# A Fourier-mixing and squared-ReLU kernel: a load issued later, a small tile in another PSUM pool, and six more pair steps without their third matmul pass

## Chip, cores and metric

The kernel runs on one core of a Trainium2 chip. The metric is the device time of one execution in microseconds; the time given for a kernel is the median of its runs. The engines are TensorE (PE, with its weight loads PEld), VectorE (DVE), ScalarE (ACT), GpSimd (POOL) and SyncE (SP). The last two only issue DMAs here, apart from some small set-up work and a few tiny copies on POOL. ScalarE also issues a few DMAs. "The queue" of an engine is its list of instructions, which it works off in order.

## What is computed

```python
# x: (8, 3008, 256), w_in: (256, 2048), w_out: (2048, 256), all float32
X = np.fft.fft(x, axis=1)
X = np.fft.fft(X, axis=2)
y = X.real.astype(np.float32).reshape(8 * 3008, 256)
h = np.maximum(y @ w_in, 0.0)
out = h * h @ w_out
```

## The kernel before

**The mathematics.** The transform along the 256 model dimensions is folded into `w_in` once, at the start: `gh[:, 0]` holds the cosine part, `gh[:, 1]` the sine part and `gh[:, 2]` is −2 times `gh[:, 1]`, one of its 128 rows (model dimension 0) being left at zero. The transform along the sequence is made with cosine and sine tables on TensorE, after "folds" on VectorE have used its symmetries. Its results are `zc` and `zs`. Rows k and S − k of the result share these: one is p + q, the other p − q, where p = `gh[:, 0]` · `zc` and q = `gh[:, 1]` · `zs`. So only half of the rows, 12,040 columns, are carried, and each column gives two rows of the output.

**Windows.** The columns are cut into 25 windows, numbered 0 to 24, in the order of the outer loop (L680). Window 0 has 240 columns, windows 2 and 3 have 376, window 5 has 448, the last has 360, all others 512. The fifth window is number 4.

**Pair steps.** A window has 8 steps, one for each pair of 128-wide chunks of the 2048 hidden features. A plain step does this: `pq` (L726) makes p + q in PSUM (L730, L731: four matmuls); `square` (L738) takes ReLU on ScalarE (L740) into a buffer `h1`, of which there are three, and squares it on VectorE (L745), or on ScalarE (L743) where the step is in `by_act`; `turn` (L733) adds −2q to the same PSUM tile (L736: two matmuls, the "third pass"); a second `square` handles the mirrored rows. So a plain step has six matmuls of 512 columns.

**Halved steps.** A step in the set `two` has no third pass. `half_q` (L751) makes q alone (L755: two matmuls), and ScalarE copies −2q to `sn` (L758). `half_p` (L760) adds p (L764: two matmuls), ScalarE copies p + q to `hd` (L767), and VectorE does the rest: a correction row times a weight (L769, twice), two additions (L770, L771), the ReLU (L773) and the square (L774) over both halves. The correction row `eb` is row 0 of `zs`, which `row_spread` (L574) sends to DRAM from ScalarE's queue (L579) and brings back to all 128 partitions from SP's queue (L581). It is issued in the last step of the window before, behind the stores that SP already has. There are two `sn` buffers, and two `hd` buffers for each of two names.

**The plan.** `plan(w)` (L666) gives the halved steps and the `by_act` steps of a window. `PLAN[4]` halves steps 1, 2, 4, 5 and gives ScalarE the first square of 0, 3, 6. `PLAN[3]` halves 1, 3, 5 and gives ScalarE 2, 4, 6. `PLAN[0]` does neither; windows 0, 1, 2 and 4 have it.

**What else runs in a step.** Between its parts each step calls `others` (L776), which runs three sorts of work.

- The second matmul `ffn2_steps` (L602) of the window before: 16 groups of 8 matmuls of 256 columns (L618), two groups a step in a full window. They read the tile `h2` that the squares wrote. Their PSUM tile `po` is in the pool `ps_o` (two banks); ScalarE copies it out (L633), and SP stores it (L598).
- The products `z_steps` (L460) for the next window: matmuls into `pz` in the pool `ps_z` (two banks), copies on ScalarE (L485, L489), and a last `scalar_tensor_tensor` on VectorE (L496), which finishes `zc` or `zs` and frees the bank.
- The folds of the batches to come. For the batch in place i, `d_even` and `n_cos` run in the window in `first_at`, steps 0 and 2 (L713). `d_odd`, `n_sin`, `odds`, `even`, `back` and `nyq` run in the next window, the one in `fold_at` (L702), and the four `late` jobs in the one in `late_at` (L710), at steps 3 to 6.

| windows | first part of a fold | second part | late part | plan before |
|---|---|---|---|---|
| 9, 12, 15, 18 | yes | | yes | 3 |
| 5, 8, 10, 13, 16, 19 | | yes | | 3 |
| 6, 21 | | | yes | 4 |
| 7 | yes | | | 4 |
| 3, 11, 14, 17, 20, 22, 23, 24 | | | | 4 |
| 4 | yes | | of the batch in place 1 | 0 |

**DMAs of a fold.** `load_x` (L118) brings a batch, 3 MB, into the one tile `xo` with one to two direct DMAs and two or three gathers, all from POOL's queue. For the last two places, some of them wait for another's landing (L143, L149). In the kernel before, `d_odd` calls it for the next batch as soon as it has read the tile (L356), in step 0 of the window in `fold_at`. In the same window `even` writes `scr` to DRAM at step 5 (L383), and `back` reads it back into `rb` at step 6 (L391, L393), in the same queue of POOL, behind the load. `nyq` (L372) runs after step 7: two tiny matmuls into `py`, a tile of the pool `ps_o`, and a copy by VectorE (L377).

**Pairs.** A window that has 512 columns after one of fewer than 384 treats its steps two by two (`ng` = 2, L790). Windows 1 and 4 are such.

Of the kernel before, what the change touches and what calls it, by code (L numbers as in the profile page):

```python
# [8 lines left out]
F32 = mybir.dt.float32  # L9
F16 = mybir.dt.float16  # L10
# [5 lines left out]
P = 128  # L16
# [12 lines left out]
def kernel(  # L29
# [15 lines left out]
    B, S, D = x.shape  # L45
# [9 lines left out]
    WN = 512  # L55
# [4 lines left out]
    PLAN = {4: ((1, 2, 4, 5), (0, 3, 6)), 3: ((1, 3, 5), (2, 4, 6)), 2: ((1, 4), (0, 3, 6)), 0: ((), ())}  # L60
# [42 lines left out]
    tmp = ctx.enter_context(tc.tile_pool(name="tmp", bufs=2))  # L103
# [9 lines left out]
    ps_o = ctx.enter_context(tc.tile_pool(name="ps_o", bufs=2, space=bass.MemoryType.PSUM))  # L113
# [52 lines left out]
    xs = {0: load_x(0)}  # L166
# [117 lines left out]
    at = const.tile([P, 2, P + 1], F32, name="at")  # L284
# [51 lines left out]
    def fold_steps(i):  # L336
# [16 lines left out]

        def d_odd():
            nc.vector.tensor_tensor(fof[:, :, 1:129], lo, hi, op=ALU.subtract)
            if i + 1 < B:  # L356
                xs[i + 1] = load_x(i + 1)

        def n_cos():
# [11 lines left out]

        def nyq():  # L372

            py = ps_o.tile([P, 512], F32, name="py", tag="po")
            nc.tensor.matmul(py[:, 0:1], perm[0], od[:, 0, 0, 128:129], start=True, stop=True)
            nc.tensor.matmul(py[:, 1:6], perm[1], rev_dim(od[:, 0, 1:6, 128:129], 1).rearrange("p r o -> p (r o)"), start=True, stop=True)
            nc.vector.tensor_copy(od[:, 1, :, 0:1], py[:, 0:6].rearrange("p (r o) -> p r o", o=1))  # L377
# [285 lines left out]
    for w, i in fold_at.items():  # L663
        first_at[w - 1] = i

    def plan(w):  # L666

        if w < 3 or w == 4:
            return PLAN[0]
        load = 2 * (w in fold_at) + (w in first_at) + (w in late_at)  # L670
        return PLAN[(4, 4, 3)[min(load, 2)]]

    def halved(w):

# [5 lines left out]
    for w in range(NW):  # L680
        g0, wn = wins[w]
        h2 = h2p.tile([P, NFC, 2 * WN], F16, name="h2", tag="h2")
        zcw, zsw = zwin(w)

        lo, hi = 0, NST - 1
        at = [[] for _ in range(NST)]
        post = [[] for _ in range(NST)]
        if w == 0:
            at[2] = [f0s["even"], f0s["back"]]
        elif w == 1:  # L690
            fj = fold_jobs(1)
            at = [[f] for f in fj[0:5]] + [[], [], []]
            post[5] = fj[5:6]
            lo, hi = 6, 7
        elif w == 2:
            te = table_steps(1)
            at = [[folds[1]["even"], lambda: te["freq"](), lambda: te["args"](0)], [lambda: te["turns"](0)], [lambda: te["mods"](0)],
                  [lambda: te["absm"](0)], [lambda: te["sins"](0)], [lambda: te["coss"](0)], [], [lambda: te["weigh"]()]]
            for st in range(4):
                at[st + 3] = at[st + 3] + f0s["late"][st : st + 1]  # L700
            at[7].append(folds[1]["back"])
        elif w in fold_at:  # L702
            fj = jobs_of.pop(fold_at[w])
            at = [fj[2:3], [], fj[3:4], fj[4:5], [], fj[6:7], fj[7:8], []]
            post[7] = fj[5:6]
        elif w == win_of(col_of[1, 1]) - 1:
            for st in range(4):
                at[st] = folds[1]["late"][st : st + 1]
            lo = 4
        if w in late_at:  # L710
            for st in range(4):
                at[st + 3] = at[st + 3] + folds[late_at[w]]["late"][st : st + 1]
        if w in first_at:  # L713
            fj = jobs_of[first_at[w]] = fold_jobs(first_at[w])
            at[0] = at[0] + fj[0:1]
            at[2] = at[2] + fj[1:2]
        if w == 2:
            at[2].append(row_weights)
        zj, zl = [], []
        for u in need[w + 1]:  # L720
            zu = z_steps(u)
            zj += [(zu, 0, 0), (zu, 1, 0), (zu, 0, 1), (zu, 1, 1)]
        f2 = ffn2_steps(*old) if old else []
        phs = {}

        def pq(s):  # L726
            ph = phs[s] = ps_h.tile([P, 2, 512], F32, name="ph", tag="psh")
            for a in range(2):
                f0 = (2 * s + a) * P
                nc.tensor.matmul(ph[:, a, 0:wn], gh[:, 0, f0 : f0 + P], zcw[:, 0:wn], start=True, stop=False)  # L730
                nc.tensor.matmul(ph[:, a, 0:wn], gh[:, 1, f0 : f0 + P], zsw[:, 0:wn], start=False, stop=True)  # L731

        def turn(s):  # L733
            for a in range(2):
                f0 = (2 * s + a) * P
                nc.tensor.matmul(phs[s][:, a, 0:wn], gh[:, 2, f0 : f0 + P], zsw[:, 0:wn], start=False, stop=True, skip_group_check=True)  # L736

        def square(s, sg):  # L738
            h1 = h1p.tile([P, 2, 512], F16, name="h1", tag="h1")
            nc.scalar.activation(h1[:, :, 0:wn], phs[s][:, :, 0:wn], AF.Relu)  # L740
            hv = rev_dim(h1[:, :, 0:wn], 2) if sg else h1[:, :, 0:wn]
            if sg == 0 and s in by_act:
                nc.scalar.activation(h2[:, 2 * s : 2 * s + 2, 0:wn], hv, AF.Square)  # L743
            else:
                nc.vector.tensor_tensor(h2[:, 2 * s : 2 * s + 2, sg * wn : (sg + 1) * wn], hv, hv, op=ALU.mult)  # L745

        two = halved(w)
        by_act = plan(w)[1]
        sns, hds = {}, {}

        def half_q(s):  # L751
            ph = phs[s] = ps_h.tile([P, 2, 512], F32, name="ph", tag="psh")
            for a in range(2):
                f0 = (2 * s + a) * P
                nc.tensor.matmul(ph[:, a, 0:wn], gh[:, 1, f0 : f0 + P], zsw[:, 0:wn], start=True, stop=True)  # L755
            i = ROT[0] % 2
            sn = sns[s] = const.tile([P, 2, 2, WN], F16, name=f"sn{i}", tag=f"w16_{i}")
            nc.scalar.activation(sn[:, 0, :, 0:wn], ph[:, :, 0:wn], AF.Copy, bias=0.0, scale=-2.0)  # L758

        def half_p(s):  # L760
            ph, sn = phs[s], sns[s]
            for a in range(2):
                f0 = (2 * s + a) * P
                nc.tensor.matmul(ph[:, a, 0:wn], gh[:, 0, f0 : f0 + P], zcw[:, 0:wn], start=False, stop=True, skip_group_check=True)  # L764
            hd = tmp.tile([P, 2, 2 * WN], F16, name="hd", tag=("tt", "tm")[ROT[0] % 2])
            ROT[0] += 1
            nc.scalar.activation(hd[:, :, 0:wn], ph[:, :, 0:wn], AF.Copy, bias=0.0, scale=1.0)  # L767
            for a in range(2):
                nc.vector.tensor_scalar(out=sn[:, 1, a, 0:wn], in0=eb[w][:, 0:wn], scalar1=wv[:, 2 * s + a : 2 * s + a + 1], scalar2=None, op0=ALU.mult)  # L769
            nc.vector.tensor_tensor(sn[:, 0, :, 0:wn], sn[:, 0, :, 0:wn], sn[:, 1, :, 0:wn], op=ALU.add)  # L770
            nc.vector.tensor_tensor(rev_dim(hd[:, :, wn : 2 * wn], 2), hd[:, :, 0:wn], sn[:, 0, :, 0:wn], op=ALU.add)  # L771
            hv = hd[:, :, 0 : 2 * wn]
            nc.vector.tensor_scalar(out=hv, in0=hv, scalar1=0.0, scalar2=None, op0=ALU.max)  # L773
            nc.vector.tensor_tensor(h2[:, 2 * s : 2 * s + 2, 0 : 2 * wn], hv, hv, op=ALU.mult)  # L774

        def others(s):  # L776
            for j in at[s]:
                j()
            for j in spread(f2, s, NST):
                j()  # L780
            for j in post[s]:
                j()
            if s == lo:
                zl[:] = [j for zu, part, h in zj for j in zu(part, h)]
            if s >= lo:
                for j in spread(zl, s - lo, hi - lo) if s < hi else []:
                    j()


        ng = 2 if w == 0 or wins[w - 1][1] < 384 < wn else 1  # L790
        for s0 in range(0, NST, ng):
            ss = range(s0, s0 + ng)
            if s0 in two:
                half_q(s0)
                others(s0)
                half_p(s0)
                continue
            for s in ss:
                pq(s)
            for s in ss:  # L800
                square(s, 0)
            if s0 == hi and w + 1 < NW and halved(w + 1):
                row_spread(w + 1)
            others(s0)
            for s in ss:
                turn(s)
            for s in ss:
                square(s, 1)
            for s in ss[1:]:
                others(s)  # L810
            if s0 < hi <= s0 + ng - 1 and w + 1 < NW and halved(w + 1):
                row_spread(w + 1)
        old = (w, h2)
# [32 lines left out]
```

## Time and profile before

| what | value |
|---|---|
| median of three runs | 614.8 us (614.04 to 614.96) |
| the profiled run | 615.19 us |
| its span, from the first to the last instruction | 612.8 us |
| TensorE clock granted | 0.999 |
| halved steps | 74 |

The chain that ended last, by engine and by its largest lines:

```profile
PE 61%; DVE 16%; ACT 10%; issue 5%; DMA 4%; SPq 2%; POOL 1%; DVEq 0%; ACTq 0%; POOLq 0%
PE po L618 36%; PE ph L736 5%; PE ph L730 5%; PE ph L731 5%; ACT h L740 4%; PE ph L764 3%; PE ph L755 3%; DVE h L774 3%; DMA eb<-zr 3%; DVE hd L773 2%; DVE hd L771 2%; SPq L598 2%; PE pz L480 2%; DVE h L745 2%; ACT sn L758 2%
```

Where the windows lie can be read from TensorE's timeline, by the first L730 of each eighth step:

| window | begins at, us | length, us | first step, us | last square after the next window's begin, us |
|---|---|---|---|---|
| 4 | 94.6 | 22.44 | in pairs | 0.85 |
| 6 | 139.0 | 23.66 | 2.57 | 3.73 |
| 7 | 162.7 | 25.52 | 4.40 | 2.44 |
| 9 | 211.3 | 24.95 | 3.20 | 2.00 |
| 10 | 236.3 | 24.47 | 3.20 | 1.95 |
| 12 | 285.5 | 23.06 | 3.04 | 2.01 |
| 13 | 308.6 | 24.47 | 3.20 | 1.95 |
| 15 | 357.9 | 23.06 | 3.04 | 2.01 |
| 16 | 380.9 | 24.47 | 3.20 | 1.95 |
| 17 | 405.4 | 24.78 | 3.20 | 5.19 |
| 18 | 430.2 | 25.61 | 5.59 | 2.01 |
| 19 | 455.8 | 24.47 | 3.20 | 2.69 |
| 20 | 480.3 | 26.08 | 4.50 | 2.01 |
| 21 | 506.3 | 23.05 | 3.04 | 3.22 |
| 22 | 529.4 | 24.73 | 3.61 | 2.41 |

The last column compares VectorE's last square (L745) of a window with TensorE's first matmul of the next. In a line of a timeline or of the costliest groups, the first number is a start (or, in groups, the busy time), then come the duration, engine, line, operation, the tiles written and read, their shapes, a count of merged instructions, and in brackets the idle time of that engine just before and who ended it. `SPq` is the queue of SP, whose time goes into issuing DMAs. Where "issue" stands in a chain of waits, the engine waited for nothing that the profile shows.

### The profile page before, as it was taken

How to read it: one execution, taken by the hardware profiler on the slowest of the kernel's cores; microseconds unless marked ns; L12 is line 12 of the kernel's file. 1: busy time of each engine (PE TensorE's matmuls, PEld its weight loads, DVE VectorE, ACT ScalarE, POOL GpSimd, SP SyncE). 2: the span in 40 equal slices, each digit the busy share in tenths (PEclk: the TensorE clock that was granted, in tenths of full speed). 3: DMA queues.
4: the chain of work that ended last, by engine and by line, in shares of the span. 5: the costliest groups of instructions: out<-in, count | busy, mean ns of one | idle time of the engine just before them, and what ended most of it. 6: DMA issues, size and time to landing. Idle time of an engine off the chain costs nothing.

```text
span 612.8 us, 11635 instructions
## 1 busy us (share of the span) xinstructions
PE 589.3 (96%) x4416; PEld 424.8 (69%) x4416; DVE 495.4 (81%) x838; ACT 517.3 (84%) x673; POOL 82.5 (13%) x125
## 2 busy tenths in 40 slices
PE   5799999999999999999999999999899999999997
PEld 2456776776677777777777777776577667677786
DVE  7887679696999898968987898858987697887880
ACT  7687788898898898998989889898789888898872
POOL 5343100012002202020023001220010200000000
PEclk9999999999999999999999999999999999999999
DMA  8927221183114623631155121551112311211112
GB/s 146 217 68 148 61 73 35 42 177 81 52 42 90 167 59 68 151 91 55 51 112 136 58 61 48 105 146 55 48 33 64 122 35 48 57 46 44 60 56 66
DMA packets 39592, 50.21 MB, mean 82 GB/s; under 512 B 4572, under 2 KB 33393, under 8 KB 39537
## 3 DMA queue, kind: packets, MB, share of 16 engines
q0 software_dynamic: 9344, 22.14, 18.0%
q1 hardware_dynamic: 29923, 27.11, 15.1%
q8 instruction: 34, 0.56, 0.4%
q10 hardware_dynamic: 270, 0.23, 0.1%
q14 instruction: 21, 0.17, 0.1%
HBM read 36.29 MB, written 27.86 MB: 105 GB/s over the span
## 4 chain that ended last, share of the span: by engine, by line
PE 61%; DVE 16%; ACT 10%; issue 5%; DMA 4%; SPq 2%; POOL 1%; DVEq 0%; ACTq 0%; POOLq 0%
PE po L618 36%; PE ph L736 5%; PE ph L730 5%; PE ph L731 5%; ACT h L740 4%; PE ph L764 3%; PE ph L755 3%; DVE h L774 3%; DMA eb<-zr 3%; DVE hd L773 2%; DVE hd L771 2%; SPq L598 2%; PE pz L480 2%; DVE h L745 2%; ACT sn L758 2%
## 5 line engine op out<-in xcount | busy, mean ns | idle before, releaser
L618 PE MATMUL po<-wout,h 128*128 128x256 f16 (+1 forms) x3024 | 362.2, 273 | 3.2 <-DVE od L377 1.1
L618 PEld LDWEIGHTS <-h 128*128 128x128 f16 (+1 forms) x3024 | 296.4, 98 | 75.3 <-DVE h L745 1.8
L740 ACT ACTIVATE h<-ph 128x1024 f16<-128x1024 f32 (+4 forms) x252 | 235.6, 962 | 28.6 <-PE ph L736 15.5
L745 DVE TENSOR_TENSOR h<-h 128x1024 f16<-128x1024 f16 (+4 forms) x189 | 118.1, 641 | 56.1 <-ACT h L740 47.9
L731 PE MATMUL ph<-zs,gh 128*128 128x512 f16 (+4 forms) x252 | 90.9, 363 | 1.2 <-DVE zs L496 0.9
L730 PE MATMUL ph<-zc,gh 128*128 128x512 f16 (+4 forms) x252 | 91.0, 363 | 1.1 <-ACT h L740 0.8
L774 DVE TENSOR_TENSOR h<-hd 128x2048 f16<-128x2048 f16 (+3 forms) x74 | 87.9, 1188 | 2.5
L767 ACT ACTIVATE hd<-ph 128x1024 f16<-128x1024 f32 (+3 forms) x74 | 73.6, 994 | 15.0 <-PE ph L764 14.6
L633 ACT ACTIVATE osb<-po 128x512 f32<-128x512 f32 (+3 forms) x95 | 54.9, 581 | 28.4 <-PE po L618 21.5
L758 ACT ACTIVATE sn<-ph 128x1024 f16<-128x1024 f32 (+3 forms) x74 | 73.4, 992 | 0.0
L736 PE MATMUL ph<-zs,gh 128*128 128x512 f16 (+4 forms) x252 | 69.9, 363 | 2.1 <-ACT h L740 1.0
L743 ACT ACTIVATE h<-h 128x1024 f16<-128x1024 f16 (+3 forms) x63 | 64.8, 1029 | 2.0
L771 DVE TENSOR_TENSOR hd<-hd,sn 128x1024 f16<-128x1024 f16 (+3 forms) x74 | 49.8, 673 | 19.4 <-ACT hd L767 13.4
L770 DVE TENSOR_TENSOR sn<-sn 128x1024 f16<-128x1024 f16 (+3 forms) x74 | 49.8, 673 | 7.4 <-ACT hd L767 0.5
L773 DVE TENSOR_SCALAR hd<-hd 128x2048 f16<-128x2048 f16 (+3 forms) x74 | 49.9, 675 | 2.5
L769 DVE TENSOR_SCALAR sn<-eb,wv 128x512 f16<-128x512 f16 (+3 forms) x148 | 44.6, 343 | 8.2 <-DMA eb<-zr 8.2
L764 PE MATMUL ph<-zc,gh 128*128 128x512 f16 (+3 forms) x148 | 42.8, 370 | 2.6 <-ACT sn L758 1.8
L731 PEld LDWEIGHTS <-gh 128*128 128x128 f16 x252 | 24.6, 98 | 27.4 <-issue 2.5
L730 PEld LDWEIGHTS <-gh 128*128 128x128 f16 x252 | 24.5, 97 | 26.5 <-issue 1.7
L755 PE MATMUL ph<-zs,gh 128*128 128x512 f16 (+3 forms) x148 | 42.9, 371 | 0.0
L423 POOL COPY xt<-xt 128x2 f16<-128x2 f16 x16 | 5.6, 379 | 215.4 <-DVE xt L406 215.4
L736 PEld LDWEIGHTS <-gh 128*128 128x128 f16 x252 | 23.2, 97 | 9.6 <-issue 4.3
(121 smaller groups left out, 377.7 us busy)
## 6 DMA issues: line engine op xcount, KB each, us to landing
out_dram<-osb SPq DMA_DIRECT2D x77, 128.0 KB
xo<-in_x_dram POOLq DMA_DIRECT2D x7, 768.0 KB
scr<-ev POOLq DMA_DIRECT2D x8, 390.0 KB, 3.9
eb<-zr SPq DMA_DIRECT2D x18, 128.0 KB
rb<-scr POOLq DMA_DIRECT2D x16, 130.0 KB
out_dram<-osb SPq DMA_DIRECT2D x12, 94.0 KB
w<-in_moe_w_in_dram POOLq DMA_DIRECT2D x2, 512.0 KB
wout<-in_moe_w_out_dram POOLq DMA_DIRECT2D x1, 1024.0 KB
```

The costliest lines, as they stand in the source:

```text
L618: nc.tensor.matmul(po[0:m, j * D : (j + 1) * D], h2[:, fc, q : q + m], wout16[:, fc, :], start=(fc == 0), stop=(fc == NFC - 1))
L730: nc.tensor.matmul(ph[:, a, 0:wn], gh[:, 0, f0 : f0 + P], zcw[:, 0:wn], start=True, stop=False)
L731: nc.tensor.matmul(ph[:, a, 0:wn], gh[:, 1, f0 : f0 + P], zsw[:, 0:wn], start=False, stop=True)
L736: nc.tensor.matmul(phs[s][:, a, 0:wn], gh[:, 2, f0 : f0 + P], zsw[:, 0:wn], start=False, stop=True, skip_group_check=True)
L740: nc.scalar.activation(h1[:, :, 0:wn], phs[s][:, :, 0:wn], AF.Relu)
L743: nc.scalar.activation(h2[:, 2 * s : 2 * s + 2, 0:wn], hv, AF.Square)
L745: nc.vector.tensor_tensor(h2[:, 2 * s : 2 * s + 2, sg * wn : (sg + 1) * wn], hv, hv, op=ALU.mult)
L758: nc.scalar.activation(sn[:, 0, :, 0:wn], ph[:, :, 0:wn], AF.Copy, bias=0.0, scale=-2.0)
L767: nc.scalar.activation(hd[:, :, 0:wn], ph[:, :, 0:wn], AF.Copy, bias=0.0, scale=1.0)
L771: nc.vector.tensor_tensor(rev_dim(hd[:, :, wn : 2 * wn], 2), hd[:, :, 0:wn], sn[:, 0, :, 0:wn], op=ALU.add)
L773: nc.vector.tensor_scalar(out=hv, in0=hv, scalar1=0.0, scalar2=None, op0=ALU.max)
L774: nc.vector.tensor_tensor(h2[:, 2 * s : 2 * s + 2, 0 : 2 * wn], hv, hv, op=ALU.mult)
```

## The change

- `d_odd` issues the next load only for the places 0 and 1. For later ones a table `load_at` issues it in step 1 of the window after `fold_at`, or, where that next window already holds the first part of the next fold (place 3, window 8), in step 0 of the same window, as before.
- `py` of the places 2 and later is taken from the pool `ps_z` under the name `pz`.
- `plan` gives every window from 3 on `PLAN[4]`, and `PLAN[3]` only where a fold's second part runs. So windows 9, 12, 15 and 18 go from three halved steps to four. Window 4 gets the halved steps 4 and 5 and the `by_act` steps 2 and 6. The halved steps go from 74 to 80, the `by_act` steps from 63 to 65.
- In a window with paired steps, the halved steps of a pair now run as q, q, the other work of the first, p, p, the other work of the second. The counter that picks the `sn` buffer advances in `half_q`, and the name of the `hd` buffer goes by the parity of the step.

```diff
         def d_odd():
             nc.vector.tensor_tensor(fof[:, :, 1:129], lo, hi, op=ALU.subtract)
-            if i + 1 < B:
+            if i < 2 and i + 1 < B:
                 xs[i + 1] = load_x(i + 1)
...
-            py = ps_o.tile([P, 512], F32, name="py", tag="po")
+            py = (ps_z if i > 1 else ps_o).tile([P, 512], F32, name="py", tag="pz" if i > 1 else "po")
...
+    load_at = {}
+    for w, i in fold_at.items():
+        if i + 1 < B:
+            load_at[w if w + 1 in first_at else w + 1] = (i + 1, 0 if w + 1 in first_at else 1)
+
     def plan(w):
 
-        if w < 3 or w == 4:
+        if w < 3:
             return PLAN[0]
-        load = 2 * (w in fold_at) + (w in first_at) + (w in late_at)
-        return PLAN[(4, 4, 3)[min(load, 2)]]
+        if w == 4:
+            return (4, 5), (2, 6)
+        return PLAN[3 if w in fold_at else 4]
...
+        if w in load_at:
+            i, s = load_at[w]
+            at[s] = at[s] + [lambda i=i: xs.__setitem__(i, load_x(i))]
...
             i = ROT[0] % 2
+            ROT[0] += 1
             sn = sns[s] = const.tile([P, 2, 2, WN], F16, name=f"sn{i}", tag=f"w16_{i}")
...
-            hd = tmp.tile([P, 2, 2 * WN], F16, name="hd", tag=("tt", "tm")[ROT[0] % 2])
-            ROT[0] += 1
+            hd = tmp.tile([P, 2, 2 * WN], F16, name="hd", tag=("tt", "tm")[s % 2])
...
             if s0 in two:
-                half_q(s0)
+                for s in ss:
+                    half_q(s)
                 others(s0)
-                half_p(s0)
+                for s in ss:
+                    half_p(s)
+                for s in ss[1:]:
+                    others(s)
                 continue
```

## The prediction

> **What bounds the kernel now.** I read the page first, then TensorE's timeline window by window, then VectorE's in the windows where the change adds work, then the chain of waits where TensorE stood still.
>
> ```profile
> PE 589.3 (96%) x4416; PEld 424.8 (69%) x4416; DVE 495.4 (81%) x838; ACT 517.3 (84%) x673; POOL 82.5 (13%) x125
> ```
>
> TensorE is the bound on average. Its timeline at the start of window 12 gives its prices:
>
> ```profile
> 285.54 0.38 PE L730 MATMUL ph<-zc,gh 128*128 128x512 f16 x1
> ...
> 288.58 0.59 PE L755 MATMUL ph<-zs,gh 128*128 128x512 f16 x2
> ...
> 291.20 0.38 PE L730 MATMUL ph<-zc,gh 128*128 128x512 f16 x1
> ```
>
> From start to start, a plain pair step takes 288.58 − 285.54 = 3.04 us and a halved one (no third pass) 291.20 − 288.58 = 2.62. The windows are these steps end to end almost without a gap, so a halved step is worth 0.42 us, as long as nothing else is late. TensorE stood still for more than half a microsecond in few places after window 2; two matter here, at the starts of windows 18 and 20:
>
> ```profile
> 433.10 0.61 PE L618 MATMUL po<-wout,h 128*128 128x256 f16 x4 [0.81 <-DVE h L774]
> 434.82 0.39 PE L618 MATMUL po<-wout,h 128*128 128x256 f16 x2 [1.11 <-DVE h L745]
> ...
> 482.42 1.91 PE L618 MATMUL po<-wout,h 128*128 128x256 f16 x16 [1.14 <-DVE od L377]
> ```
>
> In each case VectorE was behind. The first step of window 18 took 5.59 us for 3.04, a loss of 2.55; that of window 20 took 1.30 too long. The chain of waits says why VectorE was behind in window 17:
>
> ```profile
> 403.60 2.72 SPq L598
> ...
> 406.65 1.63 SPq L598
> ...
> 408.39 7.07 DMA eb<-zr
> 415.48 0.63 DVE sn L769 x2
> ```
>
> Stores kept SP busy, the row `eb` left at 408.39, landed at 415.46, and VectorE had waited 4.94 us for it. Its last square of window 17 ended 5.19 us after window 18 began; in undisturbed windows that figure is 2.0. So TensorE tolerates 5.19 − 2.55 = 2.64. Window 21 checks it: its last square ended 3.22 after window 22 began, so 0.58 is due, and the first step there took 3.61 against 3.20 in like windows.
>
> Now VectorE in window 12, which has the first part of one fold and the late part of another (windows 9, 15 and 18 are alike):
>
> ```profile
> 288.38 0.21 DVE L350 COPY xo<-xo 1x256 f16<-1x256 f16 x1
> ...
> 297.21 0.61 DVE L769 TENSOR_SCALAR sn<-eb,wv 128x512 f16<-128x512 f16 x2
> ...
> 301.31 0.69 DVE L406 TENSOR_TENSOR xt<-rb 128x1040 f16<-128x1040 f16 x1
> ...
> 307.31 1.28 DVE L745 TENSOR_TENSOR h<-h 128x1024 f16<-128x1024 f16 x2
> 309.92 0.69 DVE L745 TENSOR_TENSOR h<-h 128x1024 f16<-128x1024 f16 x1 [1.32 <-ACT h L740]
> ```
>
> No line from 288.38 to 307.31 has an idle time: VectorE is already full there, and 1.32 us before the last square is all the room it has. A halved step costs it 301.31 − 297.21 = 4.10, a square 0.60.
>
> **The change, part by part.**
>
> *A fourth halved step in windows 12, 15 and 18.* TensorE saves 0.42 in each. VectorE gets 4.10 and loses two squares, 0.60 for one, 0.47 for the other (`d_even` starts earlier, but the square behind it then waits for ScalarE, which in like windows ends at 4.4 us into the window): +3.03. ScalarE trades two passes of 0.96 for two of 0.99, nothing. VectorE's chain ended its second-last square at 307.31 + 1.20 = 308.51; now 308.51 + 3.03 = 311.54, and the last, no longer waiting, at 312.23. Window 13 would start at 308.60 − 0.42 = 308.18, so the last square is 4.05 late, 1.41 over the tolerance. Net 1.41 − 0.42 = +1.0 each, **+3.0** for three. Bounds: −0.4 each if the lag is absorbed; +1.6 if squares that hold their h1 buffers longer also cost TensorE some 0.6 inside the window.
>
> *The same in window 9.* VectorE idles 0.52, 0.20 and 0.98 there, so of 3.03 at least 1.33 is left over. What is late next is `zs` (L496), which window 10 needs at once:
>
> ```profile
> 235.24 0.60 DVE L496 SCALAR_TENSOR_TENSOR zs<-es,pz 128x133 f16<-128x133 f32 x2
> ```
>
> It would end at 235.84 + 1.33 = 237.17, against a need at 236.3 − 0.42 + 0.22 = 236.1. Stall 1.1 to 2.8 (no idle time absorbed); I take 1.3, near the low end, since the 0.98 is surely absorbed. Net **+0.9**.
>
> *Two halved steps in window 4* (steps 4 and 5, as a pair). TensorE saves 4 matmuls of 0.215 = 0.86. VectorE has 8.06 us between the end of the second `yt` there (107.05) and the `zc` it must finish (115.11); it now has to fit 2 × 4.10 + 0.60 = 8.80 in, and loses some 1.0 more because the first `hd` comes only after two copies `sn` (0.91 each), an `es` (0.40) and its own copy on ScalarE. `zs` then ends near 107.05 + 8.80 + 1.0 + 1.06 = 117.9, where window 5 would want it at 117.25 − 0.86 = 116.4. Stall 1.5, net **+0.7**; bounds −0.86 (all hidden) and +1.0. The row `eb` for window 4 is one more DMA pair; its wait on ScalarE's queue is inside the upper bound.
>
> *The loads.* In the folds of i = 2, 4, 5 and 6 the load's three DMAs (four and five for the last two batches) move behind `scr` and `rb` in POOL's queue; for i = 3 nothing moves. Behind them POOL holds only the small copies L423 to L425 of the late part, a window later or, in window 6, four steps later. The tile that a load overwrites has long been read, so each load starts when `rb` is issued, some 4 us into the next window, and takes 10 us (19.4 for the last batch, from 385.8 to 405.2 with its waits). It is wanted at the start of the window after, 15 us or more later, for the last one about 5. So the loads themselves cost nothing. What they free: the last load filled 393 to 405 while the stores ahead of window 17's `eb` were stuck. Without it SP should reach `eb` by about 405 and window 17 starts on time: **−2.55** (0 if the stores are slow by themselves, as those ahead of window 19's `eb` are with no load near).
>
> What the loads hit next: the last load then runs from about 407 to 427, into window 17's stores and the `eb` of window 18, which landed at 435.48, just when a window 18 begun on time wants it (430.2 + 5.5). The view by stretches shows the DMA engines 7% busy from 427 to 431, one of sixteen: the tail of stores is served by one engine. Any delay there falls on the one window with no room on VectorE, so it costs in full. Bounds: 0 (the load is over before the stores of 418 come) and 4.9 (the wait seen in window 17). I take the middle, **+2.5**.
>
> [...]
>
> *py in the z pool.* It removes the wait on `od` L377 at 482.42; VectorE's lag is then within what TensorE tolerates (2.69 after window 20 began). **−1.2**, between −1.3 and 0. Elsewhere ScalarE waited for `py` 0.5 us at a time beside its own slack: nothing. The z bank it borrows is released by an L496 of an earlier step: nothing. The counter and the buffer names: nothing, two buffers each stay a step or more apart.
>
> Sum: 3.0 + 0.9 + 0.7 − 2.55 + 2.5 − 1.2 = +3.35. The profiled run took 615.19 for its span of 612.8; against the median of 614.8 that makes **618.2 us**, its own range 615 to 621.5.
>
> **The rivals.**
>
> 1. *Window 18's eb is on time.* For: the DMA engines are only 16% busy from 418 to 424. Against: the stores there already ran into 431. Sum 0.85: 615.7.
> 2. *Window 17's eb stays late.* For: window 19's is late with no load. The 2.55 is then not freed, and the lag that goes into window 18 hides some or all of the 2.5 there: 618.2 to 620.7, the middle 619.5.
> 3. *A load comes too late for `d_even`.* For: one gather at 44.11 took 4.84 us on POOL where others took 1.3. Against: it is the only such one of 17. Two such gathers make the last load 7 us longer, 427 + 7 against a need at 430.2 + 2.3, so 1.5 more, 619.7, or 622 with the stores slowed as well. [...]
>
> 4. *The other side: VectorE's lag never reaches TensorE.* It decides at the 2.64 us: if the last squares of windows 9, 12, 15 and 18 come before that, six third passes are saved whole. 2.5 + 2.55 + 1.2 = 6.3 less, 608.5. For it: idle time of VectorE summed over all windows is large (19%). Against it: none of that lies in window 12 behind 288.38, and 1.4 would have to vanish.
>
> **How the numbers follow.** Forecast 0.48; rivals 0.16, 0.12, 0.07, 0.17. The range leaves out most of rival 4 and the end of 3: 613.0 to 622.5. A change within 0.2% (1.2 us, about what can be told from no change) comes from most of rival 1 and the low edge of the forecast: 0.16. Faster: rival 4 and a little of 1, 0.18. Slower 0.66.
>
> **What would show it.** Right: windows 12, 15 and 18 begin as before but their successors' first step takes 1.4 longer than 3.2; L731 of window 10 and of window 5 waits for `zs`; no wait for L377 at window 20; no wait for `eb` in window 17, one in 18. Wrong: first steps of windows 13 and 16 at 3.2, or VectorE idle inside window 12.

## The result, and the profile after

The median is 623.65 us over four runs (622.19 to 625.76). The kernel before, run beside it, has 614.5 (614.04 to 614.96). The ratio is 1.0151, with a 95% interval from 1.0119 to 1.0184: the change made the kernel slower, by more than twice what was forecast. The profiled run took 622.98 us for a span of 620.9, which is 8.1 more than the span before.

In the changed kernel the line numbers move: `pq` is L739 and L740, `turn` L745, ReLU L749, the squares L752 (ScalarE) and L754 (VectorE), `half_q` L764, the copy `sn` L768, `half_p` L774, `hd` L776, and VectorE's halved work L778 to L783. L618, L480 and L496 stay.

The page of the changed kernel: busy times, the chain that ended last, and two of the costliest groups (their last column is the idle time ahead of them).

```profile
PE 590.7 (95%) x4404; PEld 424.1 (68%) x4404; DVE 509.4 (82%) x860; ACT 518.9 (84%) x675; POOL 78.2 (13%) x125
...
PE 50%; DVE 20%; ACT 12%; issue 9%; DMA 7%; POOL 1%; DVEq 0%; SPq 0%; ACTq 0%; POOLq 0%
...
L618 PE MATMUL po<-wout,h 128*128 128x256 f16 (+1 forms) x3024 | 363.4, 273 | 5.5 <-DVE h L754 2.8
...
L778 DVE TENSOR_SCALAR sn<-eb,wv 128x512 f16<-128x512 f16 (+3 forms) x160 | 48.3, 344 | 6.3 <-DMA eb<-zr 6.3
```

Twelve matmuls fewer, yet TensorE is busy for 1.4 us more: some of its work ran at a lower clock, 0.50 from 466 to 468 us. VectorE has 14.0 us more work, and the chain passes through it for 20% of the span where it was 16%.

Windows, cut as in the table of before, against the forecast:

| stretch | length before, us | after, us | difference | forecast |
|---|---|---|---|---|
| window 4 | 22.44 | 24.03 | +1.59 | +0.7 |
| 9 and 10 | 49.42 | 51.08 | +1.66 | +0.9 |
| 12 and 13 | 47.53 | 48.81 | +1.28 | +1.0 |
| 15 and 16 | 47.53 | 48.81 | +1.28 | +1.0 |
| 17 to 19 | 74.86 | 77.97 | +3.11 | −2.55 + 2.5 + 1.0 |
| 20 | 26.08 | 24.78 | −1.30 | −1.2 |
| start and tail | | | +0.5 | 0 |

They sum to 8.1. The same places in TensorE's timeline of the changed kernel; the brackets hold TensorE's idle time and what ended it:

```profile
96.22 0.38 PE L739 MATMUL ph<-zc,gh 128*128 128x512 f16 x1 [0.85 <-ACT h L749]
...
104.70 0.59 PE L745 MATMUL ph<-zs,gh 128*128 128x512 f16 x2 [0.94 <-ACT h L749]
...
116.20 0.59 PE L745 MATMUL ph<-zs,gh 128*128 128x512 f16 x2 [0.56 <-ACT h L749]
...
239.23 0.38 PE L740 MATMUL ph<-zs,gh 128*128 128x512 f16 x1 [1.42 <-DVE zs L496]
...
302.43 0.59 PE L774 MATMUL ph<-zc,gh 128*128 128x512 f16 x2 [0.21 <-ACT sn L768]
...
315.11 0.39 PE L618 MATMUL po<-wout,h 128*128 128x256 f16 x2 [0.93 <-DVE h L754]
...
463.57 0.61 PE L618 MATMUL po<-wout,h 128*128 128x256 f16 x4 [2.62 <-DVE h L783]
465.12 0.60 PE L618 MATMUL po<-wout,h 128*128 128x256 f16 x2 [0.93 <-DVE h L754]
```

The first three lie in window 4 and wait for ScalarE. 239.23 is window 10's first step, 315.11 window 13's, the last two window 19's; all wait for VectorE. 302.43 is a small wait in the second half of window 12, which matters below.

Why window 19 lost most is in the chain of waits ahead of it (start, duration, what):

```profile
405.33 6.80 DMA scr<-ev
...
417.22 6.33 DMA xo<-in_x_dram,idx_f
...
426.68 10.85 DMA xo<-in_x_dram,idx_r
...
437.76 6.17 DMA eb<-zr
```

The last load began at 417.22, 6.3 us into window 17, which begins at 410.91 here; the prediction had it at 407, 1.6 us into the window of the kernel before. `scr` was 6.8 us under way, and `rb`, which takes POOL another 4.2 us to issue, could go only behind it. The load ran into window 17's stores, `eb` for window 18 left at 437.76, and VectorE stood 3.27 us:

```profile
443.96 0.62 DVE L778 TENSOR_SCALAR sn<-eb,wv 128x512 f16<-128x512 f16 x2 [3.27 <-DMA eb<-zr]
```

The view by stretches then shows something new. After start and length come the busy times, and ahead of the last two columns the granted TensorE clock:

```profile
464.00:466.00 2.00, 1.07 (x7) 0.73 (x6) 2.00 (x4) 1.02 (x1) 1.10 (x2) 0.79 0.45 138
466.00:468.00 2.00, 2.00 (x8) 0.80 (x6) 2.00 (x3) 1.08 (x2) 0.00 (x0) 0.50 0.07 24
468.00:470.00 2.00, 2.00 (x19) 1.70 (x18) 1.89 (x4) 0.87 (x2) 0.00 (x0) 0.86 0.08 24
```

For 3.4 us from 465.15, as the three shares of the clock add up, TensorE ran at half its clock. From 465.12 to the `half_p` at 469.96 it took 4.84 us; the same instructions of window 13, from 315.11 to 318.40, took 3.29. So the clock cost 1.55.

### The profile page after: what moved, and what is told of

Same layout as the page of the kernel before. It is cut to its first block, busy times and chain, and to the rows that moved or that the text cites. A ratio compares the mean times of both kernels' runs of the same rounds, so it can differ in the third digit from the quotient of the medians.

```text
span 620.9 us, 11635 instructions
## 1 busy us (share of the span) xinstructions
PE 590.7 (95%) x4404; PEld 424.1 (68%) x4404; DVE 509.4 (82%) x860; ACT 518.9 (84%) x675; POOL 78.2 (13%) x125
## 4 chain that ended last, share of the span: by engine, by line
PE 50%; DVE 20%; ACT 12%; issue 9%; DMA 7%; POOL 1%; DVEq 0%; SPq 0%; ACTq 0%; POOLq 0%
PE po L618 28%; ACT h L749 5%; PE ph L745 4%; DVE h L783 4%; PE ph L739 4%; PE ph L740 4%; PE ph L774 3%; DVE hd L782 3%; DVE hd L780 3%; PE ph L764 3%; DVE sn L779 2%; DVE h L754 2%; ACT sn L768 2%; PE pz L480 2%; DMA xo<-in_x_dram,idx_r 2%
## 5 line engine op out<-in xcount | busy, mean ns | idle before, releaser
L618 PE MATMUL po<-wout,h 128*128 128x256 f16 (+1 forms) x3024 | 363.4, 273 | 5.5 <-DVE h L754 2.8
L618 PEld LDWEIGHTS <-h 128*128 128x128 f16 (+1 forms) x3024 | 296.4, 98 | 78.9 <-DVE h L754 4.0
L749 ACT ACTIVATE h<-ph 128x1024 f16<-128x1024 f32 (+4 forms) x240 | 223.6, 959 | 25.7 <-PE ph L745 10.5
L754 DVE TENSOR_TENSOR h<-h 128x1024 f16<-128x1024 f16 (+4 forms) x175 | 108.3, 638 | 49.7 <-ACT h L749 48.6
L783 DVE TENSOR_TENSOR h<-hd 128x2048 f16<-128x2048 f16 (+3 forms) x80 | 95.2, 1190 | 2.7
L776 ACT ACTIVATE hd<-ph 128x1024 f16<-128x1024 f32 (+3 forms) x80 | 79.7, 998 | 20.6 <-PE ph L774 20.2
L740 PE MATMUL ph<-zs,gh 128*128 128x512 f16 (+4 forms) x240 | 86.4, 362 | 2.7 <-DVE zs L496 2.3
L739 PE MATMUL ph<-zc,gh 128*128 128x512 f16 (+4 forms) x240 | 86.4, 362 | 1.7 <-ACT h L749 1.4
L768 ACT ACTIVATE sn<-ph 128x1024 f16<-128x1024 f32 (+3 forms) x80 | 79.6, 996 | 0.5 <-PE ph L764 0.5
L780 DVE TENSOR_TENSOR hd<-hd,sn 128x1024 f16<-128x1024 f16 (+3 forms) x80 | 54.0, 675 | 21.9 <-ACT hd L776 15.9
L745 PE MATMUL ph<-zs,gh 128*128 128x512 f16 (+4 forms) x240 | 67.3, 364 | 3.6 <-ACT h L749 3.0
L752 ACT ACTIVATE h<-h 128x1024 f16<-128x1024 f16 (+3 forms) x65 | 66.9, 1030 | 2.1
L779 DVE TENSOR_TENSOR sn<-sn 128x1024 f16<-128x1024 f16 (+3 forms) x80 | 54.0, 675 | 7.6
L778 DVE TENSOR_SCALAR sn<-eb,wv 128x512 f16<-128x512 f16 (+3 forms) x160 | 48.3, 344 | 6.3 <-DMA eb<-zr 6.3
L774 PE MATMUL ph<-zc,gh 128*128 128x512 f16 (+3 forms) x160 | 46.2, 371 | 3.3 <-ACT sn L768 2.4
L764 PE MATMUL ph<-zs,gh 128*128 128x512 f16 (+3 forms) x160 | 46.7, 375 | 0.0
L739 PEld LDWEIGHTS <-gh 128*128 128x128 f16 x240 | 23.4, 97 | 26.8 <-issue 3.4
L740 PEld LDWEIGHTS <-gh 128*128 128x128 f16 x240 | 23.4, 97 | 26.7 <-issue 3.1
L745 PEld LDWEIGHTS <-gh 128*128 128x128 f16 x240 | 22.2, 98 | 11.1 <-issue 6.4
L764 PEld LDWEIGHTS <-gh 128*128 128x128 f16 x160 | 15.6, 98 | 17.9 <-issue 0.5
```

The source lines that it names most:

```text
L618: nc.tensor.matmul(po[0:m, j * D : (j + 1) * D], h2[:, fc, q : q + m], wout16[:, fc, :], start=(fc == 0), stop=(fc == NFC - 1))
```

## The experiments

Each was profiled and, but for the one with four h1 buffers, timed against the kernel before on the same chip. Executions of one kernel differ by some us (611.16 to 614.35 in the first experiment); the lengths of windows that nothing disturbs repeat to some 0.02 us, so most readings are of windows.

**The changed kernel with the plan of before.** `plan` and so the halved steps are put back; the loads and `py` stay changed.

> The changed kernel with the plan of before (74 halved steps, none in window 4): only the loads and py are changed. If the six added halved steps overload VectorE and ScalarE, the losses of windows 4, 9/10, 12/13 and 15/16 (1.59, 1.66, 1.28, 1.28 us) go, window 18 has room again for most of the 3.3 us wait for its eb, and the time falls from 623 to 612.5 to 614.5, at or a little under the kernel before; the wait for L377 at window 20 stays away. If the moved loads are what costs, it stays above 619. [...]

Measured: 611.86 us (611.16 to 614.35, five runs), ratio 0.9939 (0.9913 to 0.9965). Windows 4, 9, 10, 12, 13, 15 and 16 are as before the change. Window 17 still waits 0.72 us for `eb`, window 18 3.10, but window 19's first step is 4.18 in place of 7.84. The two other parts of the change are a gain; the plan turned it into a loss.

**The plan alone.** The kernel before with the new plan, the pairs and the buffer names; loads and `py` old.

> The kernel before with the plan, the paired halved steps and the buffer names of the changed one; loads and py as before. If the plan is the loss, windows 4, 9/10, 12/13 and 15/16 lose 1.6, 1.7, 1.3 and 1.3 as in the changed kernel, window 17's eb is late as before (2.5 at window 18's start), window 18 is overloaded on top (1.3 at window 19): 621 to 623. If the moved loads are the loss, at most 617.

Measured: 623.11 us (622.38 to 624.57), ratio 1.0121 (1.0093 to 1.0148). Windows 4, 10, 13 and 16 are exactly as in the changed kernel. `eb` is 5.15 us late in window 17, window 18's first step takes 5.92, and the half clock comes there, at 441.2.

**The last load where it was.**

```diff
-            if i < 2 and i + 1 < B:
+            if (i < 2 or i == B - 2) and i + 1 < B:
...
-        if i + 1 < B:
+        if i + 2 < B:
             load_at[...] = ...
```

> The changed kernel with the last load alone put back to where it was (behind d_odd in window 16). If that load's traffic in window 17 makes window 18's eb late, VectorE waits less than 0.5 us for that eb (3.3 in the changed kernel) and window 19's first step falls from 7.84 to about 4.5; in exchange window 17's eb is some 5 us late again and window 18's first step loses about 2.5. Sum: 621 to 622.5. If the stores make it late by themselves, window 18's eb stays 3 us late and the time rises to 624 or more.

Measured: 623.18 us (621.53 to 626.59), ratio 1.0107 (1.008 to 1.0133), no different from the changed kernel. Window 17's `eb` is 5.68 us late, window 18's on time: lengths 25.15, 27.66 and 25.77 for windows 17 to 19, a sum of 78.58 against 77.97. With the stores as they are, the load makes late whichever `eb` it meets, at about the same price.

**`py` alone.** The kernel before with only `py` in the z pool.

> The kernel before with py in the z pool and nothing else that takes time. If the bank was what held TensorE at the start of window 20, its first step falls from 4.50 to 3.2 and the time by 1.3 us (ratio 0.998), window 17's and 19's eb as late as before. If VectorE's lag behind it (2.69 us) holds TensorE all the same, the step stays at 4 or more and the time does not move.

Measured: 613.47 us (612.48 to 615.44, ten runs), ratio 0.9968 (0.995 to 0.9985). Window 20's first step falls from 4.50 to 3.20. TensorE's timeline there shows the second matmul, L618, with no wait ahead of it:

```profile
482.31 0.38 PE L741 MATMUL ph<-zs,gh 128*128 128x512 f16 x1
482.53 1.91 PE L618 MATMUL po<-wout,h 128*128 128x256 f16 x16
```

**Window 4 without ScalarE's squares.**

```diff
-            return (4, 5), (2, 6)
+            return (4, 5), ()
```

> The changed kernel, window 4 with the halved steps 4 and 5 but no by_act steps. If ScalarE's order is what costs there (its squares of steps 2 and 6 stand between the two ReLUs of a pair), TensorE's waits of 0.94 and 0.56 us go and window 4 falls from 24.03 to 22.6 to 23.0 us. If VectorE is what costs (as the forecast had it), the two squares that come back to it, 1.2 us, make window 4 or window 5's first step longer: 24.0 to 25. In the whole time 1.2 us either way, 621.5 to 624.

Measured: 623.16 us, ratio 1.0116 (1.0093 to 1.0138), hardly another time; the windows tell more. Window 4 falls from 24.03 to 22.22, below the 22.44 of before, and window 5 grows by 0.47 to 22.44, its first step now waiting for ScalarE's ReLU, which waits 1.33 us for VectorE's work. So the two squares on ScalarE cost window 4 1.81, and what the prediction named, VectorE's lag at the begin of window 5, is worth 0.47. The two windows together are 0.25 longer than before: the two halved steps bring nothing there in either form.

**The late part of the last folds a window earlier.** This takes VectorE's work out of windows 12, 15 and 18.

```diff
-        late_at[win_of(col_of[i, 1]) - 2] = i
+        late_at[win_of(col_of[i, 1]) - (3 if i > 3 else 2)] = i
```

> The changed kernel with the late part of the folds in places 4 to 7 one window earlier (windows 11, 14, 17, 20, where VectorE has 6 us of idle time), so that windows 12, 15, 18 and 21 lose 2.1 us of VectorE's work each. If VectorE's sum of work is what overloads them, the first steps of windows 13 and 16 fall from 4.5 to 3.2, window 19's from 7.84 to about 5.5, window 10's stays at 5.0 (place 3 is not moved): 616.5 to 618.5 us. If it is the buffers between the engines (sn, hd) and not the work, windows 13 and 16 stay above 4 us and the time above 621.

Measured: 618.88 us (618.51 to 618.98), ratio 1.0061 (1.0042 to 1.0081). Windows 13 and 16 are back at 24.47, their first steps at 3.20: it was VectorE's sum of work that was late there. But window 12 is 23.74 long and 15 is 23.65, both longer than the 23.06 of before. That excess lies in their first two steps: the last squares of windows 11 and 14, where the late part has gone, now end 3.1 and 3.0 us after the next window's begin, where it was 2.0. From step 2 on the windows are as in the changed kernel, within 0.05 us: step 4, the added halved one, takes 2.98 us here too, where an undisturbed one takes 2.62. So the fourth halved step brings next to nothing even when VectorE has room behind it.

**ScalarE's squares 0, 6, 7 in place of 0, 3, 6** in windows 9, 12, 15 and 18, which asks why that is so.

```diff
+        if w in (9, 12, 15, 18):
+            return PLAN[4][0], (0, 6, 7)
```

> The changed kernel with the by_act steps 0, 6, 7 in place of 0, 3, 6 in windows 9, 12, 15 and 18; VectorE's work is the same, one square comes earlier and one goes. Theory (the fourth third pass brought nothing there because ScalarE's square in step 3 stands ahead of its copy sn of step 4, for which L774 waits): the length of windows 12, 15 and 18 falls from 23.05 to 22.7, and VectorE, with the same sum of work, ends as late as in the changed kernel, so window 13's first step is between 3.9 and 4.9. Rival (something else holds step 4): 23.05. About 621 in all by the theory, if window 19's stall is as in the changed kernel, 622.5 by the rival.

Measured: 622.24 us (621.3 to 622.52), ratio 1.0109 (1.0075 to 1.0144). Windows 12 and 15 are 22.75 long, 0.30 less, as the theory had it, and window 13's first step is 4.18. What the changed kernel did on ScalarE in window 12:

```profile
299.00 1.06 ACT L752 ACTIVATE h<-h 128x1024 f16<-128x1024 f16 x1
299.97 0.58 ACT L633 ACTIVATE osb<-po 128x512 f32<-128x512 f32 x1
300.44 1.02 ACT L749 ACTIVATE h<-ph 128x1024 f16<-128x1024 f32 x1
301.35 1.03 ACT L768 ACTIVATE sn<-ph 128x1024 f16<-128x1024 f32 x1
```

The square of step 3 (299.00) stands ahead of the copy `sn` of step 4, and `half_p` at 302.43 waits for that copy to end. Without that square, in TensorE's timeline of this run, `half_p` goes without a wait:

```profile
302.94 0.59 PE L776 MATMUL ph<-zc,gh 128*128 128x512 f16 x2
```

The 0.30 was not worth its price: window 10 became 27.16 long, 0.86 more, with `zs` later still.

**A fourth square on ScalarE**, by_act (0, 3, 6, 7) in the same four windows.

```diff
+        if w in (9, 12, 15, 18):
+            return PLAN[4][0], (0, 3, 6, 7)
```

> The changed kernel, windows 9, 12, 15 and 18 with the first square of step 7 on ScalarE too: VectorE has 0.6 us less to do in each. If VectorE's last square sets when the next window goes on, the first steps of windows 13 and 16 fall from 4.5 to 3.9. If it is the h1 buffer freed by the square of step 6 (ScalarE's ReLU of the next window waits for it), they stay within 0.1 of 4.5; window 10 (held by zs) stays at 5.0 or gets worse. 621.5 to 623.5 us.

Measured: 618.53 us (617.22 to 621.48), ratio 1.006 (1.0031 to 1.0089). Window 13's first step is 3.27, window 16's 3.26: neither of the numbers expected. VectorE's last square still ends 3.5 us after window 13 has begun, and yet TensorE doesn't wait at all. Its timeline, then VectorE's:

```profile
315.20 1.97 PE L618 MATMUL po<-wout,h 128*128 128x256 f16 x16
```

```profile
316.55 1.89 DVE L756 TENSOR_TENSOR h<-h 128x1024 f16<-128x1024 f16 x3
```

The code says why. In its first four steps a window's second matmul reads only the unmirrored half of `h2`. So the first square of step 7 is what TensorE needs, in its fifteenth matmul; the mirrored one is wanted half a window later. Given to ScalarE, the first square is there in time, and what VectorE owes behind step 5 isn't wanted yet. (In window 19 of this run, with `eb` late, VectorE is behind with step 5 itself, and TensorE waits 2.63 us for that.) In the changed kernel four squares run from 313.77 at 0.6 us each, the first of step 7 is the second of them, and TensorE goes on at 315.11, just behind it. The run before this one agrees: in its timeline of TensorE, window 13 waits after ten matmuls, for the halved step 5 (L785), and not for step 7.

```profile
312.93 1.26 PE L618 MATMUL po<-wout,h 128*128 128x256 f16 x10
314.99 0.83 PE L618 MATMUL po<-wout,h 128*128 128x256 f16 x6 [0.80 <-DVE h L785]
```

**Four h1 buffers.** In the changed kernel the first ReLU of window 13 also waits, 1.71 us, for an `h1` buffer that VectorE has not yet freed. Which of the two holds TensorE?

```diff
-    h1p = ctx.enter_context(tc.tile_pool(name="h1p", bufs=3))
+    h1p = ctx.enter_context(tc.tile_pool(name="h1p", bufs=4))
...
-    osp = ctx.enter_context(tc.tile_pool(name="osp", bufs=3))
+    osp = ctx.enter_context(tc.tile_pool(name="osp", bufs=2))
```

> The changed kernel with four h1 buffers in place of three, and two osb buffers in place of three to make room. Read in windows 12 to 16 alone. Theory 1 (TensorE waits for the last square, which its second matmul reads): the last square is as late as before and window 13's first step stays at 4.5. Theory 2 (the first ReLU of the window waits for an h1 buffer that VectorE has not freed, and that wait is what makes TensorE late): with the fourth buffer that ReLU takes one freed long ago, and the first step is 3.2 to 3.7.

Measured: window 13's first step 4.39, window 16's 4.38. TensorE's wait is the same to the hundredth, though ScalarE now runs the two ReLUs at once (TensorE's timeline, then ScalarE's):

```profile
322.60 0.39 PE L618 MATMUL po<-wout,h 128*128 128x256 f16 x2 [0.93 <-DVE h L754]
```

```profile
319.29 1.94 ACT L749 ACTIVATE h<-ph 128x1024 f16<-128x1024 f32 x2
```

So the square holds TensorE, and a fourth buffer is worth 0.1. The whole took 631.65 us, one run; windows 8, 11 and 18, with two `osb` buffers, became 2.1 to 4.3 us longer, which says nothing on this question.

**Stores cut in two.** The stores are 1 to 128 rows long, many not a multiple of 16. Here each is cut into a multiple of 16 and the rest.

```diff
-            eng.dma_start(
-                out=bass.AP(tensor=out.tensor, offset=out.offset + row * D, ap=[[kstep * D, cnt], [1, D]]),
-                in_=osb[lo : lo + cnt, :])
+            for a, n1 in ((0, cnt - cnt % 16), (cnt - cnt % 16, cnt % 16)):
+                if n1:
+                    eng.dma_start(
+                        out=bass.AP(tensor=out.tensor, offset=out.offset + (row + kstep * a) * D, ap=[[kstep * D, n1], [1, D]]),
+                        in_=osb[lo + a : lo + a + n1, :])
```

> The changed kernel with each output store cut into a multiple of 16 rows and a rest of under 16. If stores of a prime number of rows make a tail on one DMA engine that delays eb, VectorE's waits for eb in windows 17 and 18 (1.07 and 3.27 us) go, window 19's first step falls from 7.84 to about 4.5, its half-clock stretch with it: 618 to 619.5 us. If the last load's own traffic delays eb, the wait in window 18 stays over 2 us and the time over 621.5.

Measured, on the changed kernel: 617.93 us (616.59 to 619.84, eight runs), ratio 1.0041 (1.0024 to 1.0059). From window 6 on none waits for `eb` any more, 18 is 23.05 long and 19 is 25.76, and the half clock in the middle is gone (the eight runs have a mean granted clock of 0.994 to 1.0, the four of the changed kernel 0.991 to 0.996). Windows 4, 10, 13 and 16 keep their losses.

**The cut stores without the plan**, and **the cut stores alone**:

> The changed kernel with the plan, the pairs and the buffer names of before, so only the loads and py moved, and with every store cut into a piece of a multiple of 16 rows and the rest. Theory (the row eb is late because a store whose rows are not a multiple of 16 ends on one DMA engine, and the third passes bring nothing in the fold windows): no wait for eb in windows 17, 18 and 19, first steps of windows 18, 19 and 20 at 3.04, 3.20 and 3.20, no other window moved; against the run with the old plan and whole stores (611.86) that is 25.45 - 24.47 = 1.0 us less, 610.9. Rival (the extra DMA instructions, about twice as many stores in SP's queue, delay eb by themselves): 612 or more.

> The kernel before with nothing but the cut stores. Theory (the stores are slow by themselves, and neither the moved load nor py is needed): windows 17 and 19 get eb on time, window 18 begins with 3.04 in place of 5.59 and window 20 with 3.20 in place of 4.50, since VectorE's lag there comes from the late eb: 2.55 + 1.30 less, 611.3. Rival (the last load, on the way from 393 to 405, holds the stores up whatever their shape): window 17's eb still 2 us or more late, and only window 20's 1.3 us are won: 613.5.

Measured: 610.99 us (610.2 to 612.68, seven runs), ratio 0.9933 (0.9908 to 0.9958), with the loads and `py` changed; 610.58 us (609.39 to 611.58, six runs), ratio 0.9916 (0.9889 to 0.9943), for the kernel before with nothing but the cut stores. Their windows 8 to 23 agree to 0.02 us: 17 to 20 are 24.78, 23.06, 24.47 and 24.78. For windows 6 to 19 `eb` now leaves 1.1 to 1.5 us after `zr`, where it was up to 5.0. In the kernel before, `eb` for window 17 left at 408.39, 3.0 us after the window's begin, and kept VectorE waiting 4.94 us. With the cut stores it leaves at 406.35, 0.65 us ahead of the window's begin at 407.00 (SP's timeline):

```profile
406.35 1.14 SPq L581 DMA_DIRECT2D eb<-zr  x1
```

and VectorE, when it comes to it, waits for nothing:

```profile
411.46 0.69 DVE L747 TENSOR_TENSOR h<-h 128x1024 f16<-128x1024 f16 x1 [2.51 <-ACT h L742]
412.07 0.61 DVE L771 TENSOR_SCALAR sn<-eb,wv 128x512 f16<-128x512 f16 x2
```

The last load is where it was before the change. So neither moving it nor `py` was needed: with `eb` on time, VectorE isn't late at window 20 either, and the wait for `py` is gone by itself. This version beats both kernels.

## The prediction, step by step

The sum was +3.35, the span grew by 8.1. The direction held, the size did not, and the time fell outside the range. Three steps of the prediction failed above all: the 0.42 us that a halved step was to save, with ScalarE's part put at nothing (0.01 was saved in windows 12 and 15); the sum for window 4, which had no term for ScalarE's two added squares (+1.59 for +0.7); and the sum for windows 17 to 19, which had no term for TensorE's clock (1.55).

**Right: a fourth halved step makes VectorE late in windows 12 and 15.** The last square was forecast 4.05 us after the next window's begin; it came at 4.10. The stall was forecast at 1.41, the first step grew by 1.30. The tolerance of 2.64, taken from window 18 of before, served well, although it isn't the last square that TensorE waits for but the one before it.

**Wrong: that a halved step saves 0.42.** In windows 12 and 15 it saved nothing (23.05 against 23.06), nor in 18 (23.14), in window 9 only 0.17. The working had said that ScalarE trades two passes for two and put that at nothing; it looked at ScalarE's sum and not at its order. The fourth step made `sn` of step 4 wait behind a square: the step takes 2.98 us, where an undisturbed halved step takes 2.62, which took back what the matmuls gave. In the run with squares 0, 6, 7 it takes 2.68, so 0.30 of it is shown; what holds the rest stays open. The kernel before had it in its table: window 21, with four halved steps and two matmuls fewer than window 12, is 23.05 us long, window 12 is 23.06. With 0 saved, the net is 1.28 where 1.0 was forecast.

**Window 4: the right sign for the wrong reason.** +0.7 was to come from `zs` late on VectorE. It came to +1.59 from ScalarE. Its two added squares, which stand between the ReLUs of a pair of steps, cost 1.81. At the window's begin ScalarE also stood 0.94 us until `zs` was there, which `zr`'s DMA waits for in its queue, and the window's first step grew by 0.60, with the squares or without them (ScalarE's timeline):

```profile
94.83 0.66 ACT L633 ACTIVATE osb<-po 128x256 f32<-128x256 f32 x2 [0.94 <-DVE zs L496]
```

Less the 0.86 of the matmuls, that is +1.55. "Its wait on ScalarE's queue is inside the upper bound" covered the DMA alone: the bound of +1.0 held nothing for the squares.

**Window 9: the mechanism right, the size short.** `zs` was late for window 10, as said, and the first step grew by 1.83 where 1.3 was taken, near the low end of 1.1 to 2.8. With a saving of 0.17 for 0.42 the net was 1.66, not 0.9.

**The loads: half right.** Window 17's `eb` came 1.07 us late in place of 4.94, and window 18 got its 2.5 us back, as forecast. Window 18's `eb` was late by 3.27, inside the bounds of 0 to 4.9, and pushed VectorE's last square from 4.10 to 6.83, which is 2.7 where 2.5 was taken. The 2.5 was the middle of those wide bounds, so that it came so close is luck. What failed stands beside it. "The last load then runs from about 407" puts its begin 1.6 us into window 17, though the same working has `rb` issued "some 4 us into the next window"; it began 6.3 us into it. Its last data still landed at 437.53, just ahead of `d_even` at 437.62, so rival 3 missed by 0.1 us. And no term allowed for the clock: the stall of 2.62 and the one of 0.93 behind it were followed by half clock for 3.4 us, at 1.55. So windows 17 to 19 cost 3.11, not 0.95: of the 2.16 between, 1.55 are the clock, 0.4 the third pass that was not saved, and 0.2 `eb`.

**`py`: right.** −1.30 for −1.2, and the run of that part alone shows the same 1.30. What the prediction did not see is that it removes a symptom; the lag behind it comes from window 19's late `eb`, and that from the stores.

**The rivals.** The other side, that the lag never reaches TensorE, is excluded by the waits at 315.11 and 239.23. That window 18's `eb` is on time is excluded by the 3.27. That the stores are slow by themselves was named, as the ground of rival 2, and it is the cause: with the stores cut, `eb` is on time wherever the load is issued. Where the prediction asked whether the load or the stores delay `eb`, it should have let the stores weigh more, since window 19's was late with no load near.

Most of the miss of 4.7 us in the sum is thus 2.15 in windows 17 to 19, 0.9 in window 4, 0.75 in windows 9 and 10, and 0.55 in 12, 13, 15 and 16. The range had been built on single bounds of each term; nearly all but `py` went to the dear side, and the clock was in none. The start and the tail, 0.5 of it, were not studied.

## What to carry to other kernels

A matmul that is removed is worth its time only if what follows it in another engine's order comes earlier too: look at the order of that engine's instructions in the very step, not at its sum. Where a row sent through DRAM comes late again and again, look first at the transfers ahead of it in its queue; their shape (here row counts that are not a multiple of 16) can be a cheaper cure than moving a load or easing the engine that waits. And find which write the late reader really needs: here moving one square to another engine removed the same stall as moving a whole group of jobs to another window.

## What the hardware showed

**Half the clock came after some short stalls and not after others.** Waits of 2.62 and 0.93 us, 1.55 us from the first matmul behind the one to the first behind the other, were followed by 3.4 us at half clock. So were 1.03 and 1.11 (the plan alone, window 18), and so were two single waits, of 2.46 and 2.31 (four h1 buffers, windows 11 and 18, in a run with a mean granted clock of 0.990). 0.81 and 1.11 in the kernel before were not, nor were single waits of 2.63 (the fourth square on ScalarE, window 19) and 2.29 (squares 0, 6, 7, window 10). So the length of a wait alone doesn't decide. What decides between 2.31 and 2.63 stays open.

**Stores of odd lengths held up another queue's row.** Cutting 113 rows into 112 and 1, and the others likewise, took the time from `zr` to `eb` from up to 5.0 us to 1.5 at most, although the stores become more (314 in the trace of before, 504 with the cut stores alone). The view by stretches shows the tail that goes away. The first line is of the kernel before, behind stores of window 18 and with no load under way: the DMA engines are 7% busy (the column ahead of the last) for 2.5 us. The second is the like place with the cut stores alone, 1%:

```profile
450.50:453.00 2.50, 2.50 (x22) 1.90 (x20) 2.26 (x5) 2.47 (x4) 0.04 (x1) 1.00 0.07 24
```

```profile
452.50:455.00 2.50, 2.50 (x21) 1.92 (x20) 2.35 (x4) 1.83 (x3) 1.10 (x2) 1.00 0.01 2
```

The 7% is the work of about one of sixteen, by estimate; the view gives the mean of all sixteen and doesn't tell which of them worked, so that one engine serves the tail, as the prediction has it, is the author's estimate. Why a row count that is not a multiple of 16 makes a store slow is not shown.

And the stores, all in SP's queue, held up `zr`, which goes from ScalarE's. SP's waits in the changed kernel, from 415 to 440 us, have it (in all, times, longest):

```profile
SPq L581 <- DMA zr<-zs: 2.9, 1, 2.9
```

**The odd stores slowed another transfer too.** In the changed kernel `scr` took 6.8 us in window 16, 405.33 to 412.13, with no load in its way; the median of its eight is 4.3. The same kernel with the cut stores has POOL waiting 3.15 us for it in that place, where it had waited 6.77 (POOL's timelines, whole stores first):

```profile
412.71 1.10 POOL L391 DMA_DIRECT2D rb<-scr  x2 [6.77 <-DMA scr<-ev]
```

```profile
410.89 1.09 POOL L391 DMA_DIRECT2D rb<-scr  x2 [3.15 <-DMA scr<-ev]
```
